# Moving group 4's attention output from TensorE to the crossbar, and groups 3 and 4 one unit earlier, in a fused window-attention and SwiGLU kernel

## The chip, the cores and the metric

The kernel runs on one core of one Trainium2 chip. The metric is the device time of one execution in microseconds (us), as the median of several runs. The kernel before takes 239.64 us (five runs, 239.41 to 241.12).

## The reference

Two layers are fused. The first is attention with a sliding window and attention sinks, for 4 batches, 8 heads, 768 tokens and a head width of 64. A query sees the first four keys of its sequence (the sinks) and the 128 most recent keys:

```python
keep = is_sink | in_window          # pos < 4, or 0 <= query - key < 128
a = softmax(where(keep, q @ k.T / 8, -1e9))
x = (a @ v) as [3072 tokens, 512]
```

The second is a SwiGLU block on these 3072 tokens, with a model width of 512 and an inner width of 1536:

```python
g = x @ w_gate
out = (g * sigmoid(g) * (x @ w_val)) @ w_out
```

## The kernel before

**Groups and blocks.** Attention runs over 12 groups of 256 tokens; group g is the third `g % 3` of batch `g // 3`. The SwiGLU block runs over eight token blocks of `SIZES` 256, 256, 256, 512, 512, 512, 512, 256 tokens. Block 3 holds groups 3 and 4, block 4 groups 5 and 6, block 5 groups 7 and 8, and so on. Blocks 0 and 1 share one 512-token buffer, under the name "01".

**The steps of a group g.**

- `load_nat(g)` (line 111) loads k and q in four DMAs from the POOL queue, `load_v(g)` (line 122) loads v in two. `NV(g)` is both. From group 4 on the loaded k and q lie in a buffer with a single copy (`natp`, one buffer), so that the load of the next group must wait until this group's k and q have been read.
- `xbar(g)` (line 259) reads them: four DMA transposes from the SP queue, through the crossbar, which write `kT` and `qT`. Groups 2 and 3 are transposed on TensorE instead (`TN`, line 245), groups 0 and 1 in other ways on TensorE.
- `Ss(g)` are two steps `step_S` (line 292): the scores of four heads each, 8 or 12 matmuls into four PSUM banks, four exponentials on ScalarE (line 299) and two masks on VectorE (line 304), which are put off until the next `flush`.
- `K(g)` is `step_K` (line 320): the scores against the sinks, for the groups that are not the first of their batch, and one exponential (line 324) that writes `es`.
- `PVs(g)` are four steps `step_PV` (line 355). The first one of a group that is not the first of its batch also issues the sinks' part for all four (line 335, `o<-vsb,es`), which reads `es`. VectorE then normalises (lines 363 and 369) into `xn`.
- `Xs(g)` are two steps `step_X`: 128 tokens of `xn` are transposed into `xT`, the input of the SwiGLU block. For groups in `PEX` TensorE does it in four matmuls (line 396, tile `px`) and VectorE or ScalarE copies the result; for the others it is one DMA transpose from the SP queue (line 391).

**Units.** The SwiGLU work is cut into units. A `gate` unit of a 512-token block is one slice f of 128 inner columns: four matmuls with the gate weights, a tanh on ScalarE, four matmuls with the value weights (all line 417), and two products on VectorE (lines 445 and 451). For a 256-token block a unit holds two slices, in matmuls of 256 columns. A `down` unit is 12 matmuls for 128 tokens (line 492), an eviction on ScalarE (line 497) and a store from the SP queue (line 500). In a gate unit the attention steps that are assigned to it come between the gate and the value matmuls; in a down unit they are spread over the 12 matmuls.

**The order is written by hand.** `weave` walks through a list of units and looks up each unit's attention steps in `slots`; a slot number is the index of the unit. Every engine works through its own instructions in this order, and so do the DMA queues of SP and POOL. The first weave holds the blocks 0, 1 and 2: slots 0 to 11 are the gates of blocks 0 and 1, 12 to 17 the gates of block 2, 18 and 19 the downs of block 0, 20 and 21 those of block 1, 22 and 23 those of block 2. The second weave holds block 3 (slots 0 to 11 gates, 12 to 15 downs), the third block 4, and so on. `pair(ga, gb)` places two groups in one weave.

Of the kernel before, what the change touches and what calls it, by code (L numbers as in the profile page):

```python
# [14 lines left out]
def kernel(  # L15
# [12 lines left out]
    nc = tc.nc  # L28
# [9 lines left out]
    DFC = DF // P  # L38
# [3 lines left out]
    SIZES = [256, 256, 256, 512, 512, 512, 512, 256]  # L42
    assert sum(SIZES) == NTOK and NG == 12
    OFF = [sum(SIZES[:i]) for i in range(len(SIZES))]
    PEX = (0, 1, 2, 4)

    VS = 72
    FCH = [2] * 6
# [108 lines left out]
    warmed = const.tile([P, 1], FP32)  # L157
# [49 lines left out]
    kTs, qTs, es_t, e_t, xns, xTs = {}, {}, {}, {}, {}, {}  # L207
# [171 lines left out]
    def step_X(g, j, evict="v"):  # L379
# [6 lines left out]
        elif tb > 1 and off == 0:  # L386
            xTs[tb] = dense(xtp.tile([P, DMC * 512], BF16, tag="xT", name="xT"),
                            DMC, SIZES[tb])
        if g not in PEX:
            def sp():  # L390
                nc.sync.dma_start_transpose(xTs[tb][:, :, off:off + P], xns[g, j])
# [110 lines left out]
    def gates(tb):  # L502
        return [(gate, tb, f) for f in range(0, DFC, 512 // SIZES[tb])]

    def downs(tb):
        return [(down, tb, t) for t in range(SIZES[tb] // P)]

    def A(fn, *a):
        return lambda: fn(*a)

    def TN(g, evict="av"):
        return [A(step_TN, g, i, j, evict) for j in range(2) for i in range(2)]

    def Ss(g):
        return [A(step_S, g, p2) for p2 in range(2)]

    def PVs(g):
        return [A(step_PV, g, j, hh) for hh in range(2) for j in range(2)]

    def Xs(g):  # L520
        return [A(step_X, g, j) for j in range(2)]

    def K(g):
        return A(step_K, g)

    def weave(us, slots):
        assert all(i < len(us) for i in slots)
        for i, (fn, tb, x) in enumerate(us):
            fn(tb, x, slots.get(i, []))

    def slots(*pairs):
        sl = {}
        for at, steps in pairs:
            for i, step in zip(at if isinstance(at, tuple) else (at,) * len(steps),
                               steps):
                sl.setdefault(i, []).append(step)
        return sl
# [81 lines left out]
    for i in range(4):  # L619
# [26 lines left out]
    flush()  # L646

    g0, g1, g2 = gates(0), gates(1), gates(2)
    us = [(gate_held, *g0[0][1:]), (gate_first, *g0[1][1:]), g1[0], g1[1], g0[2], g1[2],
          *((gate, "01", f) for f in range(6, DFC)),  # L650
          *g2, *downs(0), *downs(1), *downs(2)]

    def L(*fs):
        def f():
            for x in fs:
                x()
        return f

    def NV(g):
        return L(A(load_nat, g), A(load_v, g))  # L660

    weave(us, slots(
        (4, TN(2)[::2]), (5, TN(2)[1::2]), ((6, 7), Ss(2)), (6, [K(2)]),
        ((8, 8), PVs(2)[:2]), (9, [A(step_PV, 2, 0, 1, "a"), A(step_PV, 2, 1, 1, "a")]),
        ((10, 11), [A(step_X, 2, 0, "a"), A(step_X, 2, 1, "a")]),
        (11, [NV(4), lambda: nc.gpsimd.tensor_copy(out=vcl[64:128], in_=vcl[0:64])]),
        ((14, 14, 15, 15), TN(3, "aa")),
        (15, [A(xbar, 4)]), (15, [NV(5)]), (19, [A(xbar, 5)]), (19, [NV(6)]),
        (23, [A(xbar, 6)]), (23, [NV(7)]),
        ((17, 18), Ss(3)), (18, [A(step_ks, 1)]), (18, [A(step_vsb, 1)]),  # L670
        ((19, 19, 19, 20), PVs(3)), (20, Xs(3)),
        ((19, 20), Ss(4)), (19, [K(4)]),
        ((21, 21, 22, 22), PVs(4)), (22, Xs(4))))

    def pair(ga, gb, sh=0):
        s = sh
        return [((s, s + 2), Ss(ga)), (s, [K(ga)]),
                ((s + 4, s + 5, s + 6, s + 7), PVs(ga)),
                ((s + 6, s + 8), Ss(gb)), ((s + 8, s + 9), Xs(ga)), (s + 6, [K(gb)]),
                ((12, 12, 13, 13) if s else (10, 10, 11, 12), PVs(gb)),  # L680
                ((14, 14) if s else (12, 13), Xs(gb))]

    weave(gates(3) + downs(3), slots(
        (2, [A(xbar, 7)]), (2, [NV(8)]),
        (15, [A(step_ks, 2), A(step_vsb, 2)]), *pair(5, 6),
        (15, [A(xbar, 8)]), (15, [NV(9)])))
    weave(gates(4) + downs(4), slots(
        *pair(7, 8), (3, [A(xbar, 9)]), (15, [A(step_ks, 3), A(step_vsb, 3)]),
        (3, [NV(10)]), (15, [A(xbar, 10)]), (15, [NV(11)])))
    weave(gates(5) + downs(5), slots(*pair(9, 10), (6, [A(xbar, 11)])))  # L690
    us = gates(6) + gates(7) + downs(6) + downs(7)
    us[-1] = (lambda tb, t, a: down(tb, t, a, True), *us[-1][1:])
# [37 lines left out]
```

## Time and profile before

| | |
|---|---|
| median of 5 runs | 239.64 us |
| the profiled execution | 239.41 us |
| its span in the profile | 237.6 us (1.8 us lie around it) |
| mean TensorE clock granted | 0.998 of full speed |
| TensorE matmuls (PE) | 229.1 us busy, 96% of the span |
| VectorE (DVE) | 158.3 us, 67% |
| ScalarE (ACT) | 113.5 us, 48% |
| GpSimd (POOL), which issues the loads | 74.5 us, 31% |

Busy times are those of one profiled execution. Matmuls are pipelined and their ends are modelled, so the share of PE is an upper bound on its use. In the chain of waits each piece is either work or what released it; a DMA piece that runs beside busy TensorE costs only what is left when TensorE has run out of work. "Idle before" in the timeline is the time that an engine stood before an instruction, and the arrow names what ended it.

### The profile page before, as it was taken

How to read it: one execution, taken by the hardware profiler on the slowest of the kernel's cores; microseconds unless marked ns; L12 is line 12 of the kernel's file. 1: busy time of each engine (PE TensorE's matmuls, PEld its weight loads, DVE VectorE, ACT ScalarE, POOL GpSimd, SP SyncE). 2: the span in 40 equal slices, each digit the busy share in tenths (PEclk: the TensorE clock that was granted, in tenths of full speed). 3: DMA queues.
4: the chain of work that ended last, by engine and by line, in shares of the span. 5: the costliest groups of instructions: out<-in, count | busy, mean ns of one | idle time of the engine just before them, and what ended most of it. 6: DMA issues, size and time to landing. Idle time of an engine off the chain costs nothing.

```text
span 237.6 us, 4880 instructions
## 1 busy us (share of the span) xinstructions
PE 229.1 (96%) x1874; PEld 127.9 (54%) x1901; DVE 158.3 (67%) x336; ACT 113.5 (48%) x233; POOL 74.5 (31%) x98
## 2 busy tenths in 40 slices
PE   8899999999999999999999999999999999999994
PEld 5567845795555444543444454444444445488443
DVE  5887888768652888950798980588970598877000
ACT  4884485467443836412745622655622663333221
POOL 8996865720807117080352600080000000000000
PEclk9999999999999999999999999999999999999999
DMA  8999999996999999999498964599204100200132
GB/s 142 155 181 177 181 200 205 157 144 70 132 137 199 169 119 112 132 122 237 111 137 93 133 58 139 137 94 145 44 17 136 70 3 0 44 3 0 50 131 88
DMA packets 107655, 27.36 MB, mean 115 GB/s; under 512 B 94704, under 2 KB 104688, under 8 KB 107632
## 3 DMA queue, kind: packets, MB, share of 16 engines
q0 software_dynamic: 76640, 13.90, 76.9%
q1 hardware_dynamic: 30448, 12.89, 27.5%
q8 instruction: 15, 0.25, 0.4%
q10 hardware_dynamic: 544, 0.26, 0.4%
q14 instruction: 8, 0.07, 0.1%
HBM read 28.34 MB, written 6.29 MB: 146 GB/s over the span
## 4 chain that ended last, share of the span: by engine, by line
PE 84%; DMA 5%; ACT 3%; DVE 2%; POOL 2%; issue 2%; SPq 0%; POOLq 0%; DVEq 0%; ACTq 0%
PE pv L417 26%; PE pg L417 25%; PE pd L492 22%; PE o L355 4%; PE s L292 4%; DMA xT<-xn 3%; DMA va<-in_v_dram 2%; ACT e L299 2%; POOL rows L100 1%; DVE xn L369 1%; PE pn L245 1%; POOL x L188 1%; PE o L335 1%; PE pk L320 1%; ACT th L437 1%
## 5 line engine op out<-in xcount | busy, mean ns | idle before, releaser
L445 DVE SCALAR_TENSOR_TENSOR u<-th,pg 128x512 bf16<-128x512 f32 x72 | 49.1, 682 | 38.7 <-ACT th L437 38.7
L417 PE MATMUL pg<-xT,wg 128*128 128x512 bf16 (+1 forms) x351 | 73.1, 335 | 1.1 <-DMA xT<-xn 0.5
L437 ACT ACTIVATE th<-pg 128x512 f32<-128x512 f32 x72 | 43.5, 604 | 63.3 <-PE pg L417 59.6
L417 PE MATMUL pv<-xT,wv 128*128 128x512 bf16 (+1 forms) x351 | 73.1, 336 | 0.5 <-ACT e L299 0.2
L492 PE MATMUL pd<-wo,ht 128*128 128x512 bf16 (+2 forms) x291 | 64.8, 370 | 0.4
L451 DVE TENSOR_TENSOR ht<-u,pv 128x512 bf16<-128x512 bf16 x66 | 45.4, 687 | 9.8 <-PE pv L417 2.9
L417 PEld LDWEIGHTS <-wg 128*128 128x128 bf16 x360 | 35.1, 98 | 28.4 <-issue 1.3
L299 ACT ACTIVATE e<-s 128x512 bf16<-128x512 f32 (+1 forms) x88 | 42.9, 581 | 4.0 <-PE s L292 4.0
L492 PEld LDWEIGHTS <-ht 128*128 128x128 bf16 x300 | 27.9, 98 | 29.9 <-issue 0.5
L417 PEld LDWEIGHTS <-wv 128*128 128x128 bf16 x360 | 32.2, 98 | 20.5 <-issue 1.7
L111 POOL DMA_DIRECT2D nat<-in_k_dram x20 | 17.7, 888 | 76.1 <-DMA qT<-nat 73.7
L497 ACT ACTIVATE ot<-pd 128x512 f32<-128x512 f32 (+1 forms) x24 | 14.3, 596 | 47.4 <-PE pd L492 43.4
L304 DVE TENSOR_TENSOR e<-e,mask 128x1024 bf16<-128x1024 bf16 (+1 forms) x44 | 27.1, 649 | 4.0 <-ACT e L299 3.9
L122 POOL DMA_DIRECT2D va<-in_v_dram x24 | 21.5, 921 | 5.2 <-DMA wo<-in_moe_w_out_dram 2.5
L369 DVE TENSOR_TENSOR xn<-o,rcp 128x256 bf16<-128x256 f32 x45 | 19.1, 424 | 1.5
L355 PEld LDWEIGHTS <-e 128*128 128x128 bf16 x352 | 15.1, 98 | 8.0 <-DVE e L304 0.3
L111 POOL DMA_DIRECT2D nat<-in_q_dram x20 | 17.7, 898 | 1.0 <-DMA wv<-in_moe_w_val_dram 0.5
L355 PE MATMUL o<-va,e 128*128 128x65 bf16 x352 | 17.2, 194 | 0.4 <-DVE e L304 0.2
L292 PE MATMUL s<-qT,kT 64*128 64x128 bf16 (+1 forms) x240 | 12.9, 237 | 0.0
L292 PEld LDWEIGHTS <-kT 64*128 64x128 bf16 x240 | 7.7, 94 | 7.6 <-issue 6.6
L499 DVE TENSOR_SCALAR ot<-pd 128x128 f32<-128x128 f32 x1 | 0.3, 292 | 14.3 <-PE pd L492 14.3
L363 DVE RECIPROCAL rcp<-o 128x4 f32<-128x4 f32 x48 | 8.2, 174 | 1.7 <-PE o L355 1.7
(73 smaller groups left out, 91.6 us busy)
## 6 DMA issues: line engine op xcount, KB each, us to landing
out_dram<-ot SPq DMA_DIRECT2D x23, 256.0 KB
va<-in_v_dram POOLq DMA_DIRECT2D x24, 128.0 KB, 5.9
nat<-in_k_dram POOLq DMA_DIRECT2D x20, 128.0 KB, 4.7
nat<-in_q_dram POOLq DMA_DIRECT2D x20, 128.0 KB, 5.7
wg<-in_moe_w_gate_dram POOLq DMA_DIRECT2D x6, 256.0 KB, 8.0
wv<-in_moe_w_val_dram POOLq DMA_DIRECT2D x6, 256.0 KB, 8.3
wo<-in_moe_w_out_dram POOLq DMA_DIRECT2D x4, 384.0 KB, 11.1
st<-in_q_dram ACTq DMA_DIRECT2D x2, 128.0 KB
```

The costliest lines, as they stand in the source:

```text
L111: nc.gpsimd.dma_start(x[:, i, j].rearrange("p (h d) -> p h d", d=D), src[b, :, t0:t0 + P].rearrange("h p d -> p h d"))
L122: nc.gpsimd.dma_start(va[:, j, :, 0:D], v[b, :, t0:t0 + P].rearrange("h p d -> p h d"))
L292: nc.tensor.matmul(pss[2 * pp + h][:, col:col + n], kTs[b][r, p, kk:kk + P], qTs[b][r, p, qq:qq + n], start=True, stop=True)
L299: nc.scalar.activation(e_t[g][:, h0 + h, lo:512], pss[2 * pp + h][:, lo:512], AF.Exp, scale=scale)
L304: nc.vector.tensor_tensor(e, e, m[:, :, lo:512].broadcast_to([P, 2, 512 - lo]), op=ALU.mult)
L355: nc.tensor.matmul(o, l, r, start=(c == 0 and i == 0), stop=(i == len(mms) - 1), skip_group_check=True)
L369: nc.vector.tensor_tensor(xn, po[:, :, 0:D], rcp.broadcast_to([P, 4, D]), op=ALU.mult)
L417: nc.tensor.matmul(ps[:, i * n:(i + 1) * n], ws[fi][:, c, fo * P:(fo + 1) * P], xTs[tb][:, c], start=(c == 0), stop=(c == DMC - 1))
L437: nc.scalar.activation(th, pg, AF.Tanh, scale=0.5)
L445: nc.vector.scalar_tensor_tensor(u, th, 1.0, pg, op0=ALU.add, op1=ALU.mult)
L451: nc.vector.tensor_tensor(hts[tb][:, f:f + 512 // SIZES[tb]].rearrange("p a n -> p (a n)"), u, pv, op=ALU.mult)
L492: nc.tensor.matmul(po, hts[tb][:, f, ts * P:(ts + 1) * P], wos[f // n][:, f % n, lo:hi], start=(f == 0), stop=(f == DFC - 1))
```

## The change

- `PEX` loses group 4: its two output transposes become DMA transposes from the SP queue.
- In the first weave the units of slices 4 and 5 of blocks 0 and 1, each of two slices for one block of 256 tokens, become two joined units of one slice for 512 tokens.
- The steps of group 3 move up by one slot, those of group 4 by about one as well. The sink scores `K(4)` come directly after the second half of the scores of group 4, no longer after the first.
- `xbar(5)` with `NV(6)` moves from slot 19 to slot 22, so it comes after group 4's output. `xbar(6)` with `NV(7)` moves from slot 23 into slot 1 of the second weave, `xbar(7)` from slot 2 to slot 8 there.
- In the second weave the steps of group 5 and the scores of group 6 come one slot later. The value steps of group 6 go from slots 10, 10, 11, 12 to 10, 11, 11, 12, and its output stays in slots 12 and 13.
- `NV(8)` moves from slot 2 to slot 13. Ahead of it a new instruction on POOL reads one row of the last token of block 4's `xT`, so that POOL waits there for the transposed output of group 6.

```diff
-    PEX = (0, 1, 2, 4)
+    PEX = (0, 1, 2)
...
+    def behind(tb):
+
+        nc.gpsimd.tensor_copy(out=warmed[0:1], in_=xTs[tb][0:1, 0, 511:512])
...
-    us = [(gate_held, *g0[0][1:]), (gate_first, *g0[1][1:]), g1[0], g1[1], g0[2], g1[2],
-          *((gate, "01", f) for f in range(6, DFC)),
+    us = [(gate_held, *g0[0][1:]), (gate_first, *g0[1][1:]), g1[0], g1[1],
+          *((gate, "01", f) for f in range(4, DFC)),
           *g2, *downs(0), *downs(1), *downs(2)]
...
-        (15, [A(xbar, 4)]), (15, [NV(5)]), (19, [A(xbar, 5)]), (19, [NV(6)]),
-        (23, [A(xbar, 6)]), (23, [NV(7)]),
-        ((17, 18), Ss(3)), (18, [A(step_ks, 1)]), (18, [A(step_vsb, 1)]),
-        ((19, 19, 19, 20), PVs(3)), (20, Xs(3)),
-        ((19, 20), Ss(4)), (19, [K(4)]),
-        ((21, 21, 22, 22), PVs(4)), (22, Xs(4))))
+        (15, [A(xbar, 4), NV(5)]),
+        ((16, 17), Ss(3)), (18, [A(step_ks, 1), A(step_vsb, 1)]),
+        ((18, 18, 18, 19), PVs(3)), (19, Xs(3)),
+        (18, Ss(4)[:1]), (19, [L(Ss(4)[1], K(4))]),
+        ((20, 20, 21, 21), PVs(4)), (21, Xs(4)), (22, [A(xbar, 5), NV(6)])))
...
-                ((12, 12, 13, 13) if s else (10, 10, 11, 12), PVs(gb)),
-                ((14, 14) if s else (12, 13), Xs(gb))]
+                ((10, 11, 11, 12) if s else (10, 10, 11, 12), PVs(gb)),
+                ((12, 13), Xs(gb))]
...
-        (2, [A(xbar, 7)]), (2, [NV(8)]),
-        (15, [A(step_ks, 2), A(step_vsb, 2)]), *pair(5, 6),
-        (15, [A(xbar, 8)]), (15, [NV(9)])))
+        (1, [A(xbar, 6), NV(7)]), (8, [A(xbar, 7)]), *pair(5, 6, 1),
+        (13, [flush, A(behind, 4), NV(8)]),
+        (15, [A(step_ks, 2), A(step_vsb, 2), A(xbar, 8), NV(9)])))
```

## The prediction

> **What bounds the kernel now.** I read the page's busy times first, then the chain of waits, then the timelines of SP, POOL, PE and ACT around the moved steps.
>
> ```profile
> PE 229.1 (96%) x1874; PEld 127.9 (54%) x1901; DVE 158.3 (67%) x336; ACT 113.5 (48%) x233; POOL 74.5 (31%) x98
> PE 84%; DMA 5%; ACT 3%; DVE 2%; POOL 2%; issue 2%; SPq 0%; POOLq 0%; DVEq 0%; ACTq 0%
> ```
>
> TensorE is the bound. The span less PE's busy time is 8.5 us, but most of it is start and tail: the table of stages gives 0.23 us idle from 20 to 30 us, 0.25 from 58.5 to 62.9, 0.21 from 85 to 95, 0.52 from 101 to 112, 0.39 from 112 to 138, and about 2.6 us in all from 20 to 219 us. So a change that only hides waits can win some 2.6 us at most, and any new wait of PE is paid in full, because nothing later has slack to absorb it.
>
> The chain shows one large DMA piece, `105.21 6.71 DMA xT<-xn`, the last output transpose of group 6. The PE timeline tells what it costs:
>
> ```profile
> 101.84 9.66 PE L492 MATMUL pd<-wo,ht 128*128 128x512 bf16 x43
> 111.96 1.02 PE L417 MATMUL pg<-xT,wg 128*128 128x512 bf16 x4 [0.46 <-DMA xT<-xn]
> ```
>
> Four down units run under those 6.7 us; 0.46 us is left over. That wait is what holding back NV(8) can win.
>
> The change lives on two in-order DMA queues, so I took from them how long a crossbar step needs to land. First SP, then POOL, whose next load waits for the last of four transposes:
>
> ```profile
> 54.80 1.22 SPq L259 DMA_TRANSPOSE qT<-nat  x1
> 62.94 1.20 SPq L259 DMA_TRANSPOSE kT<-nat  x1
> 67.98 1.19 SPq L259 DMA_TRANSPOSE qT<-nat  x1
> 83.61 1.22 SPq L259 DMA_TRANSPOSE qT<-nat  x1
> 113.95 1.22 SPq L259 DMA_TRANSPOSE qT<-nat  x1
> ```
>
> ```profile
> 59.49 1.75 POOL L111 DMA_DIRECT2D nat<-in_k_dram  x2 [10.12 <-DMA qT<-nat]
> 72.84 1.75 POOL L111 DMA_DIRECT2D nat<-in_k_dram  x2 [8.11 <-DMA qT<-nat]
> 88.22 1.76 POOL L111 DMA_DIRECT2D nat<-in_k_dram  x2 [10.13 <-DMA qT<-nat]
> 116.96 1.76 POOL L111 DMA_DIRECT2D nat<-in_k_dram  x2 [11.17 <-DMA qT<-nat]
> ```
>
> From the issue of the last transpose to the release: 4.7 us (group 4), 4.9 (5), 4.6 (6), 3.0 (8). Four transposes with nothing to wait for issue 1.31 us apart. From a group's first load to the issue of its last transpose: 8.5 us (59.49 to 67.98), 10.8 (72.84 to 83.61), where three stores ran among them.
>
> **What the Trainium skill says.** "DMA: Bandwidth & Descriptors", section Issuing engines are not separate DMA queues: DMAs of all issuing engines run on the same 16 engines and interleave. The trace agrees: group 6's last transpose took 6.7 us beside NV(8)'s loads, where the uncrowded one of group 8 took 3.0. The same page, section Anatomy of one DMA: a DMA's wait is made on the issuing sequencer, before dispatch. It agrees: on SP, line 391 sat behind line 259's waits for loads. "TensorE: Matmul & The Clock Gate", section Part 4: a PE transpose takes about 275 ns in a kernel's context. In this trace four cost 0.22 us in the chain, 55 ns each, and I use that. Same page, Back-to-back issue gap: 262 cycles for 256 columns against 518 for 512, so joining two halves saves almost nothing; the trace's 0.87 us for eight and 0.86 for four agree.
>
> **The change part by part.** Sums are against the profiled execution, 239.41 us (237.6 and 1.8 around it), which stands 0.23 below the median.
>
> *Transposes of group 4 off PE.* 2 x 0.22 us: **-0.44**. Also two 0.42 us copies leave VectorE, which ends no wait there: 0. SP gets two transposes of 1.2 us each.
>
> *Joined units.* Eight passes, each 0.873 to 0.863 us: **-0.04** at most -0.1. VectorE's and ScalarE's instructions keep count and size. 0 for those.
>
> *Group 3 a slot sooner.* The scores in slot 16 need the copies of `TN(3)`, which end at 51.63 us; PE gets there at about 52.2. The masks of the second half end at about 57.85, and PE reaches the third value step at 57.84: 0 to 0.1. Slot 18 then holds one down bank, three value banks and four score banks, all eight of PSUM, so the next down bank may wait for a release: 0 to 0.5, I take **+0.1**.
>
> *Scores of group 4 a slot sooner.* Slot 18 starts at about 55.75 (before, 55.4; the second scores of group 3 now lie ahead of it). Ten down matmuls (2.16 us) and the value steps (0.48) put the first scores of group 4 at 58.4. The crossbar released group 4 at 59.49 by the POOL row, or 57.9 with group 8's 3.0 us. Wait 0 to 1.1, taken **+0.3**.
>
> *K(4) behind the second scores.* On ACT the four exponentials of 2.06 us now stand ahead of `es`. Before:
>
> ```profile
> 61.31 2.06 ACT L299 ACTIVATE e<-s 128x512 bf16<-128x512 f32 x4 [2.16 <-PE s L292]
> 63.24 0.31 ACT L324 ACTIVATE es<-pk 128x128 bf16<-128x128 f32 x1
> 65.13 2.06 ACT L299 ACTIVATE e<-s 128x512 bf16<-128x512 f32 x4 [1.09 <-PE s L292]
> ```
>
> There `es` was ready 3.3 us ahead of line 335 (66.87). Now: the second scores start at t, exponentials begin at t + 0.43 (61.31 less 60.88) and end at t + 2.5, `es` at t + 2.8. PE does scores 0.57, K 0.30, three matmuls 0.65, then four 0.86, and stands at the sink matmuls at t + 2.4. Wait **+0.45** (0 to 1). The gap of 0.25 before K(4) at 61.5 may close: **-0.1** (0 to -0.25).
>
> *Group 4's output by DMA.* Its last value step ends 8 down matmuls (1.73 us) ahead of slot 22, VectorE takes 0.65, the first transpose's issue 1.25: the second is issued some 5.6 us ahead of the first gate of block 3. It needs 3.1 to 4.9, with no load in the queues. **0**, hidden by the two downs of block 2; 6.7, the crowded value, would cost 1.1.
>
> *xbar(5) behind it.* SP's order is output, store of slot 21, xbar(5). The store waits for the eviction, 0.7 us after the slot's end E, and takes 0.5: the transposes start at E + 1.4, the last issues at E + 5.4, lands at E + 8.4 (3.0) or E + 10.3 (4.9). The scores of group 5, in slot 1 of the next weave, are due after two downs (5.18) and three passes of 0.86: E + 7.85. Wait **+0.55**, 0.3 to 2.4. Before, they had 3.6 us to spare (72.84 to 76.4).
>
> *NV(6), xbar(6).* POOL's loads start with that landing, 78.4 instead of 72.84; last transpose 8.5 to 9 later, landing 3.0 later: 90.2. The scores of group 6, now slot 7, are due at 91.3 (before 89.34, plus a unit of 1.73 and the shifts). Wait 0 to 2.4 (10.8 and 4.6 as group 6 had them); taken **+0.2**.
>
> *xbar(7), NV(8) and the POOL wait.* xbar(7) ends on SP near 101 (before 98.4); the outputs of groups 5 and 6 queue behind it, but the last is not ready until 103.8 anyway. It issues at 105.2 as before and lands in 3.1 uncrowded, 108.3, well ahead of 111.5: **-0.5** (0 to -0.5). POOL's one-element copy is free on its own; NV(8), NV(9) and later loads stand behind it. NV(8) starts near 108.6 instead of 100.54, so group 8 lands near 120.6; its scores are due at 125. The loads after it catch up: 0, the cover being this 4.6 us.
>
> Sum: -0.44 - 0.04 + 0.1 + 0.3 + 0.45 - 0.1 + 0.55 + 0.2 - 0.5 = +0.5, so 239.9 in a profiled execution and **240.0** as a median (half of the 0.23 added).
>
> **Rivals.** A measurement of this kernel can tell about 0.5%, 1.2 us, from no change.
>
> *The single k and q buffer gives slower.* One mechanism: xbar(5) queues behind group 4's output, so its landing frees the buffer some 5.6 us later for NV(6), and both score steps wait. For it: landings of 4.6 to 4.9 us for groups 4 to 6, 10.8 us of load and issue for group 6. Against it: the three stores that stretched group 6 don't recur. With 4.9, group 5 waits 2.4; with 10.8 and 4.6 from a start at 78.4, group 6 waits 2.4. One of them gives 241.9 to 242.2, both nearly 244. It decides once the two waits together pass 2 us; I put 242.1.
>
> *All new waits are hidden.* `es`, crossbars and banks cost nothing, and the old wait goes: -0.44 - 0.04 - 0.2 - 0.5 = -1.2, 238.2 to 238.4. For it: every new wait but one has a lower bound of 0. Against it: `es` comes after four exponentials in order.
>
> *Group 4's output lands late.* At 6.7 us it costs 1.1 at the second weave's start: 241.1 with the rest. Against it: no loads run beside it.
>
> *The hold does nothing*, because the 3 us are the crossbar's own: 240.5, within the bound.
>
> **Numbers.** The ledger's case, with the last rival, 0.52, own range 238.9 to 241.1; buffer 0.30 and late output 0.06 mostly above 240.85; hidden 0.12. Faster 0.12, same 0.52, slower 0.36. The range 238.5 to 242.4 takes in the hidden case and one late landing, and leaves out both at once.
>
> **What would show it.** Right: line 396 falls by 8 matmuls; PE waits at line 335 for `es` in slot 20; at line 292 for `kT<-nat` once or twice near 78 and 91; no wait of `pg` for `xT` at the third weave's start. Wrong: `pg` waits for `xT` near 75; group 5's scores start with no idle; waits for PSUM releases over 1 us in slots 18 to 20; or a wait at group 8's scores.

## The result, and the profile after

The changed kernel takes 239.58 us (median of 43 runs) beside 239.03 us of the kernel before (80 runs): a ratio of 1.0022, 95% interval 1.0013 to 1.0030, so 0.5 us slower. The forecast was 240.0 us and "same within 0.5%" as the likeliest case. It started from the five runs at 239.64 us; over 80 runs the kernel before came out 0.6 us lower, so it is the forecast difference, +0.5 us, that compares with the measured one. The profiled span went from 237.6 to 238.0 us. Four of the 22 executions of experiment 6 took 242.2 to 242.6 us, in a slow state whose cause no trace here shows, and are left out of its ratio.

The page of the changed kernel, first the busy times, then the chain's shares by engine:

```profile
PE 229.1 (96%) x1850; PEld 125.9 (53%) x1877; DVE 157.1 (66%) x334; ACT 113.8 (48%) x233; POOL 74.7 (31%) x99
PE 83%; ACT 4%; DMA 3%; SPq 3%; POOL 2%; issue 2%; DVE 2%; POOLq 0%; DVEq 0%; ACTq 0%
```

PE is as full as before, but DMA lost two points of the chain and SP's queue, 0% before, now has 3%. PE's timeline shows where PE stood (the last bracket is the idle time before, and what ended it):

```profile
64.37 0.29 PE L335 MATMUL o<-vsb,es 32*128 32x260 bf16 x4 [0.26 <-ACT es L324]
...
75.08 1.03 PE L417 MATMUL pg<-xT,wg 128*128 128x512 bf16 x4
...
78.89 0.56 PE L292 MATMUL s<-qT,kT 64*128 64x256 bf16 x10 [0.90 <-DMA qT<-nat]
...
92.32 0.51 PE L292 MATMUL s<-qT,kT 64*128 64x256 bf16 x8 [0.46 <-DVE rcp L363]
...
112.42 1.03 PE L417 MATMUL pg<-xT,wg 128*128 128x512 bf16 x4
```

The wait of 0.46 for group 6's output before the third weave is gone (112.42 has no bracket). In its place there are three: sinks of group 4 (0.26), scores of group 5 (0.90), scores of group 6 (0.46). The second weave starts at 75.08 us, where it started at 75.43 before:

```profile
75.43 1.03 PE L417 MATMUL pg<-xT,wg 128*128 128x512 bf16 x4
```

The third starts at 112.42, where it started at 111.96. Of the 0.35 us gained up to the second weave, 0.29 were there already at the last TensorE transposes of group 3 (49.58, before 49.87), and experiments 4 and 6 show that they are not the change's. So in these two profiles the moved steps of groups 3 and 4 gain 0.06 us, and the second weave loses 0.81.

The 0.06 us can't be told from nothing: from those transposes to the second weave PE took 25.56 us before and 25.50 after, but 25.76 and 26.17 in experiments 4 and 6, which have the same order as before in this stretch. The second weave is clearer. It takes 35.90 or 35.91 us in all five traces in which PE shows no wait for a transfer in it or at its end: experiments 2, 5 and 8, which have the changed order there, and 4 and 6, which have the order before. The changed kernel's 37.34 us is 1.4 us more, and it has two of the waits in it; the 36.53 us of the profile before is 0.6 us more, with one. So the new order of the second weave costs nothing of itself; its waits do.

The chain of waits of the changed kernel, in order of time, names the whole path into the 0.90 (columns: start, length, what):

```profile
68.59 0.42 DVE xn L369
69.02 0.08 DVE va L119
69.10 0.52 SPq L391
69.62 0.05 issue
69.72 1.22 SPq L391
70.93 0.04 issue
71.03 1.29 SPq L500
72.32 0.05 issue
72.41 1.23 SPq L259
73.64 0.05 issue
73.73 1.22 SPq L259
75.04 1.22 SPq L259
76.25 0.05 issue
76.35 2.51 DMA qT<-nat
78.89 0.56 PE s L292 x10
```

Read it backwards: group 5's scores wait for the landing of the fourth crossbar transpose; the four went out one behind the other; the first stood behind the store of slot 21 (line 500), which stood behind group 4's output (line 391). The one transfer in it, 2.51 us, is not a slow one: the same transpose took 2.5 us in experiments 1, 3 and 7 as well. The delay is that of one queue served in order.

### The profile page after: what moved, and what is told of

The parts are those of the page before. It is cut to its first block, busy times and chain, and to the rows that moved or that the text cites. A ratio compares the mean times of both kernels' runs of the same rounds, so it can differ in the third digit from the quotient of the medians.

```text
span 238.0 us, 4843 instructions
## 1 busy us (share of the span) xinstructions
PE 229.1 (96%) x1850; PEld 125.9 (53%) x1877; DVE 157.1 (66%) x334; ACT 113.8 (48%) x233; POOL 74.7 (31%) x99
## 4 chain that ended last, share of the span: by engine, by line
PE 83%; ACT 4%; DMA 3%; SPq 3%; POOL 2%; issue 2%; DVE 2%; POOLq 0%; DVEq 0%; ACTq 0%
PE pv L417 26%; PE pg L417 24%; PE pd L492 23%; PE s L292 4%; PE o L355 4%; ACT e L299 3%; DMA va<-in_v_dram 2%; SPq L259 2%; DMA qT<-nat 1%; POOL rows L100 1%; PE pn L245 1%; SPq L391 1%; POOL x L188 1%; PE o L335 1%; ACT th L437 1%
## 5 line engine op out<-in xcount | busy, mean ns | idle before, releaser
L451 DVE TENSOR_TENSOR ht<-u,pv 128x512 bf16<-128x512 bf16 x64 | 44.0, 687 | 11.0 <-PE pv L417 5.3
L417 PEld LDWEIGHTS <-wg 128*128 128x128 bf16 x352 | 34.3, 98 | 28.5 <-issue 0.6
L417 PEld LDWEIGHTS <-wv 128*128 128x128 bf16 x352 | 31.3, 98 | 20.8 <-issue 2.0
```

The lines of the kernel that those rows point to most:

```text
L417: nc.tensor.matmul(ps[:, i * n:(i + 1) * n], ws[fi][:, c, fo * P:(fo + 1) * P], xTs[tb][:, c], start=(c == 0), stop=(c == DMC - 1))
L451: nc.vector.tensor_tensor(hts[tb][:, f:f + 512 // SIZES[tb]].rearrange("p a n -> p (a n)"), u, pv, op=ALU.mult)
```

## The experiments

**1. The sink scores first.** The changed kernel, one line:

```diff
-        (18, Ss(4)[:1]), (19, [L(Ss(4)[1], K(4))]),
+        (18, Ss(4)[:1]), (19, [L(K(4), Ss(4)[1])]),
```

> The changed kernel with one edit: in slot 19 the sink scores of group 4 come ahead of the second half of its scores, not behind it. If the 0.26 us that TensorE waits at the sink matmuls of slot 20 come from the four exponentials ahead of es on ScalarE, es is ready some 1.5 us sooner, that wait goes, and the time falls by 0.2 to 0.35 us (239.2 to 239.4 where the changed kernel has 239.58); the waits of groups 5 and 6 at line 292 stay at about 0.9 and 0.5. Rival, a PSUM bank or VectorE is what holds the sinks: the wait stays, and the time with it.

Measured: ratio to the kernel before 1.0015 (0.9994 to 1.0035), against 1.0022 of the changed kernel: the 0.2 to 0.35 us that were expected can't be told from no gain. The wait at line 335 did go, so its cause is shown: on ACT `es` now ends at 62.5, ahead of the four exponentials. In PE's timeline the next wait grew:

```profile
64.25 0.29 PE L335 MATMUL o<-vsb,es 32*128 32x260 bf16 x4
...
79.10 0.56 PE L292 MATMUL s<-qT,kT 64*128 64x256 bf16 x10 [1.22 <-DMA qT<-nat]
```

The crossbar transposes of group 5 left SP no sooner (72.61, against 72.41), and PE's wait for them is 0.32 us longer. Group 6's scores (92.00) have no bracket here: their landing came sooner in this execution, though the loads of group 6 began 0.2 us later (79.61, against 79.41). In all, PE takes 25.01 us from group 3's last TensorE transposes to the second weave, against 25.50, and 37.30 for the second weave, against 37.34. So this trace has the gain of 0.26 us, with 0.16 more at group 4's scores, and it doesn't show it taken back; the ratio is too coarse to confirm it. The expectation that the other waits stay was wrong: they depend on when PE comes, and on landings that vary from execution to execution.

**2. Group 5's crossbar ahead of the store.**

```diff
-        ((20, 20, 21, 21), PVs(4)), (21, Xs(4)), (22, [A(xbar, 5), NV(6)])))
+        ((20, 20, 21, 21), PVs(4)), (21, Xs(4)), (21, [A(xbar, 5), NV(6)])))
```

> The changed kernel with group 5's four crossbar transposes (and the loads of group 6 behind them) at the end of slot 21, ahead of that slot's store on SP, not in slot 22 behind it. Theory of the single buffer and the SP order: the transposes start 1.2 to 1.4 us sooner, the 0.90 us wait at group 5's scores goes, the loads of group 6 start at about 78.0 instead of 79.4, and the 0.46 us wait at group 6's scores goes too: 1.2 to 1.4 us faster than the changed kernel, about 238.3, and 0.8 under the kernel before. Rival 1, the wait at group 6's scores is VectorE's (the trace names a reciprocal): only 0.9 goes, 0.46 stays. Rival 2, the crossbar is slow of itself: landing moves less than 0.5 us, and both waits stay.

Measured: ratio 0.9984 (0.9957 to 1.0011). By the two ratios that is 0.9 us under the changed kernel (the two intervals leave 0.05 to 1.7), less than the 1.2 to 1.4 that were expected; from the kernel before it can't be told. In the trace the second weave takes 1.43 us less. SP's timeline, then POOL's:

```profile
67.94 2.91 SPq L391 DMA_TRANSPOSE xT<-xn  x2
70.94 1.22 SPq L259 DMA_TRANSPOSE kT<-nat  x1
72.25 1.22 SPq L259 DMA_TRANSPOSE qT<-nat  x1
73.56 1.22 SPq L259 DMA_TRANSPOSE kT<-nat  x1
74.87 1.22 SPq L259 DMA_TRANSPOSE qT<-nat  x1
76.19 1.50 SPq L500 DMA_DIRECT2D out_dram<-ot  x3
```

```profile
77.97 1.75 POOL L111 DMA_DIRECT2D nat<-in_k_dram  x2 [15.83 <-DMA qT<-nat]
```

The transposes start 1.5 us sooner (70.94, not 72.41), group 6's loads 1.4 us sooner (77.97, not 79.41), and PE waits at neither score step: 77.55 and 90.55 have no bracket. For group 5 that settles the cause: PE came to its scores only 0.21 us sooner (77.55, against 77.76).

For group 6 it settles less. PE came to these scores 1.3 us sooner, too, and the last transpose of group 6 left SP 1.25 us sooner (86.70, against 87.95). What opened the gap is that the release came quicker after it: POOL went on 4.5 us after that issue, not 5.0. Yet the reciprocal on VectorE, which the trace of the changed kernel names, is not what these scores wait for. In experiment 1 they start before it has ended (92.00, against 92.09):

```profile
91.91 0.18 DVE L363 RECIPROCAL rcp<-o 128x4 f32<-128x4 f32 x1
...
92.00 0.50 PE L292 MATMUL s<-qT,kT 64*128 64x256 bf16 x8
```

So it was the landing of group 6 that PE waited for, which comes by way of the single buffer, since POOL starts the loads of group 6 only when group 5's transposes release it. But whether the wait is there at all depends on a landing that varies by half a microsecond: it is one execution's 0.46.

**3. Without the hold.** The changed kernel, with group 8's loads right behind group 7's transposes:

```diff
-        (1, [A(xbar, 6), NV(7)]), (8, [A(xbar, 7)]), *pair(5, 6, 1),
-        (13, [flush, A(behind, 4), NV(8)]),
+        (1, [A(xbar, 6), NV(7)]), (8, [A(xbar, 7), NV(8)]), *pair(5, 6, 1),
```

> The changed kernel without the hold: no POOL instruction behind group 6's output, and the loads of group 8 right behind the transposes of group 7 (slot 8). If those loads slow group 6's last output transpose as in the kernel before, it lands 2 to 4 us later than the 110.8 us of the changed kernel, and TensorE, which needs it at 112.4, waits 0.4 to 2 us at the third weave's first gate: 0.4 to 2 us slower. Rival, the transpose is not slowed: no wait there, same time within 0.1.

Measured: ratio 1.0177 (1.0136 to 1.0217). The direction held, the size did not: PE waits 3.4 us (PE timeline).

```profile
115.99 1.04 PE L417 MATMUL pg<-xT,wg 128*128 128x512 bf16 x4 [3.40 <-DMA xT<-xn]
```

Group 6's last output transpose left SP at 108.61 and released PE at 115.99, 7.4 us later; the loads of group 8 were issued from 105.06 to 110.3. And there is an after-effect. The table by stage (columns: stretch, its length, busy time and count of PE, PEld, DVE, ACT and POOL, granted clock, DMA share, GB/s):

```profile
116.00:117.00 1.00, 1.00 (x6) 0.34 (x8) 0.00 (x0) 0.00 (x0) 0.00 (x0) 0.98 1.31 327
117.00:118.00 1.00, 1.00 (x17) 0.64 (x20) 0.31 (x1) 0.94 (x2) 0.00 (x0) 0.50 1.42 173
118.00:119.00 1.00, 1.00 (x10) 0.35 (x11) 0.38 (x1) 1.00 (x3) 0.00 (x0) 0.50 1.30 148
119.00:120.00 1.00, 1.00 (x4) 0.35 (x3) 0.00 (x0) 0.83 (x3) 0.00 (x0) 0.50 1.33 260
```

The clock granted is half for at least 3 us, which by estimate (half of 3 us) costs some 1.5 us more than the wait. It is not in every execution: four of the six have a mean clock of 0.991 to 0.993 and take 243.2 to 245.0 us, the other two a mean clock of 1.0 and 242.0 and 242.5 us.

**4. The hold alone**, on the kernel before (`behind` is added as in the change):

```diff
-        (2, [A(xbar, 7)]), (2, [NV(8)]),
+        (2, [A(xbar, 7)]),
...
+        (13, [flush, A(behind, 4), NV(8)]),
```

> The kernel before with the hold alone: the loads of group 8 move from slot 2 to slot 13 of the second weave, behind a POOL read of block 4's last token; nothing else. If the hold is what removed the 0.46 us wait of TensorE for group 6's output, this kernel is 0.4 to 0.5 us faster than before (about 238.6), with the loads of group 8 starting near 108.5 and group 8's scores not waiting. Rival, the later loads make group 8 late: a wait at its scores near 125 us takes the gain back, same or slower.

Measured: ratio 0.9981 (0.9966 to 0.9996), 0.45 us faster (0.1 to 0.8 by the interval), as expected. No wait is left at the third weave's first gate. Group 8's loads start at 108.60, after the POOL read at 107.57. So one part of the change, taken alone, is a gain. The same hold is worth 0.45 us in the order before and some 3.7 us in the changed order (1.0177 less 1.0022; the two intervals leave 2.5 to 4.9), since there group 7's transposes, and with them group 8's loads, come later, next to group 6's output.

**5. Group 4 back on TensorE**, the rest as changed:

```diff
-    PEX = (0, 1, 2)
+    PEX = (0, 1, 2, 4)
```

> The changed kernel with group 4's two output transposes back on TensorE. My ledger has the transposes as 0.44 us of gain and the SP queue behind them as the loss. If SP's order is the loss, the crossbar of group 5 starts 2 us or more sooner (near 70 instead of 72.4), the waits at the scores of groups 5 and 6 (0.90 and 0.46) go, 0.44 of transposes come back: 0.8 to 0.95 us faster than the changed kernel, about 238.7. Rival: the waits come from moving xbar(5) to slot 22, not from the two transposes ahead of it; then SP issues it at the same time, the waits stay, and the kernel is 0.4 slower than the changed one.

Measured: ratio 0.9989 (0.9971 to 1.0007), 0.8 us under the changed kernel by the two ratios (their intervals leave 0.1 to 1.4), as expected. The transposes of group 5 left SP at 71.57, only 0.84 us sooner and not the 2 us expected: the store of slot 21 waits for its eviction in any case. It was enough. No bracket is left at the scores of groups 5 and 6, in part because PE arrives later by the 0.44 of the transposes (78.18 at group 5's scores). Moving the transposes off TensorE, in this order of SP, bought 0.44 us and cost more. The 0.44 can be seen apart here: from group 3's last TensorE transposes to the second weave PE takes 25.78 us, against 25.34 in experiment 2, whose work for PE in this stretch differs by these eight matmuls alone.

**6. Joined units alone**, on the kernel before:

```diff
-    us = [(gate_held, *g0[0][1:]), (gate_first, *g0[1][1:]), g1[0], g1[1], g0[2], g1[2],
-          *((gate, "01", f) for f in range(6, DFC)),
+    us = [(gate_held, *g0[0][1:]), (gate_first, *g0[1][1:]), g1[0], g1[1],
+          *((gate, "01", f) for f in range(4, DFC)),
```

> The kernel before with the joined units of slices 4 and 5 alone. By the durations of the passes this is worth 0.04 us, at most 0.1: not to be told from the kernel before (ratio within 0.002 of 1). Rival: fewer, longer matmuls free the weight loads or the exponentials of the units around them, and 0.3 us or more are won.

Measured: ratio 1.0002 (0.9984 to 1.0020). Nothing to be told from the kernel before, as expected. The last TensorE transposes of group 3 start at 49.64 here, at 49.58 in the changed kernel, and at 49.53 in experiment 4, which has no joined units; the 0.3 us by which all three lie ahead of the profile before (49.87) is therefore not theirs.

This trace also shows that the wait for group 6's output comes and goes in the order before. There is none at the third weave's first gate here; there is one at the second weave's, for the output of group 3, whose transposes left SP from 68.47 us on, while the loads of group 6 were issued from 69.62:

```profile
75.81 1.02 PE L417 MATMUL pg<-xT,wg 128*128 128x512 bf16 x4 [0.45 <-DMA xT<-xn]
```

In the changed order the output of group 3 leaves SP from 61.86 us on, and the loads of group 6 begin at 79.41; no trace of that order has this wait. The forecast didn't count that gain.

**7. Two buffers for loaded k and q**, the rest as changed:

```diff
-    natp = pool("natp", 1)
+    natp = pool("natp", 2)
```

> The changed kernel with two buffers for loaded k and q, not one; order of everything as it is. The loads of group 6 then start in slot 22 near 71 us, not at 79.4. If the single buffer is why group 6 waits, the 0.46 us wait at its scores goes; group 5's wait (0.90), which comes from SP's order, stays, and grows by up to 2 us if the loads of group 6 now slow group 5's crossbar transposes. Sum: between 0.5 us faster and 1.5 us slower than the changed kernel. Rival, the wait of group 6 is VectorE's (the reciprocal that the trace names): it stays.

Measured: ratio 1.0318 (1.0288 to 1.0347), 7 us slower than the changed kernel and far outside what I expected. The wait of group 6 did go, but a new one opened where I had expected none, at group 4's scores (PE timeline, then POOL's):

```profile
63.67 0.93 PE L292 MATMUL s<-qT,kT 64*128 64x256 bf16 x10 [4.60 <-DMA qT<-nat]
...
85.75 0.56 PE L292 MATMUL s<-qT,kT 64*128 64x256 bf16 x10 [1.05 <-DMA qT<-nat]
```

```profile
49.43 1.75 POOL L111 DMA_DIRECT2D nat<-in_k_dram  x2
51.16 1.77 POOL L111 DMA_DIRECT2D nat<-in_q_dram  x2
52.89 1.79 POOL L122 DMA_DIRECT2D va<-in_v_dram  x2
```

With a second buffer nothing holds group 5's loads back. They run from 49.43 instead of 58.95, beside group 4's four transposes, whose last one leaves SP at 54.49 and releases PE at 63.67: 9.2 us; in the changed kernel that transpose left at 54.46 and POOL went on at 58.95, 4.5 us later. After the 4.6 us wait the table by stage has PE's clock at 0.57 from 63 to 66 us. The single buffer delays, and it is also a hold: it keeps the next group's loads off this group's transposes.

**8. Experiments 1 and 2 together**, on the changed kernel.

```diff
-        (18, Ss(4)[:1]), (19, [L(Ss(4)[1], K(4))]),
-        ((20, 20, 21, 21), PVs(4)), (21, Xs(4)), (22, [A(xbar, 5), NV(6)])))
+        (18, Ss(4)[:1]), (19, [L(K(4), Ss(4)[1])]),
+        ((20, 20, 21, 21), PVs(4)), (21, Xs(4)), (21, [A(xbar, 5), NV(6)])))
```

> Both edits on the changed kernel: the sink scores ahead of the second scores of group 4, and group 5's crossbar transposes in slot 21 ahead of the store. If the waits are independent the gains add: 0.26 and 1.36 of wait gone, some 1.3 to 1.6 us under the changed kernel, 238.0 where the kernel before has 239.3 on this chip (ratio 0.995 to 0.998). Rival, one eats the other: PE is only earlier at the same landing of a load or transpose, and the ratio is that of the second edit alone, 0.998.

Measured: 238.36 us beside 239.36 of the kernel before, ratio 0.9968 (0.9951 to 0.9985); span 236.0. It beats the changed kernel by 1.3 us (0.7 to 1.9 by the two intervals), as expected, and the kernel before by 0.8 us (0.4 to 1.2). PE's timeline has no bracket at the sinks nor at either score step:

```profile
63.85 0.29 PE L335 MATMUL o<-vsb,es 32*128 32x260 bf16 x4
...
77.24 0.62 PE L292 MATMUL s<-qT,kT 64*128 64x128 bf16 x12
...
90.22 0.51 PE L292 MATMUL s<-qT,kT 64*128 64x256 bf16 x8
```

The edit whose gain could not be told by itself (1) shows in the trace here: PE is 0.31 us ahead of experiment 2 at the sinks and still at group 5's scores (77.24 against 77.55). The two ratios differ by 0.16% and their intervals overlap, so the rival, that the second edit does it all, is not excluded by the times.

## Why the prediction was right

The forecast, "same", and its sum (+0.5 us, measured +0.5) held, and the mechanism of the ledger, new waits on an SP queue that is served in order against the transposes and the old wait that go, is the one that the chain shows. The size of the sum is in part luck. Term by term, the waits by one profile each:

| term | forecast, us | measured, us | shown by |
|---|---|---|---|
| output transposes off PE | -0.44 | -0.44; 8 matmuls fewer at line 396 (24, before 32) | experiments 2 and 5 |
| joined units | -0.04 | ratio 1.0002 alone | experiment 6 |
| PSUM release in slot 18 | +0.1 | no such wait in the trace | profile |
| group 4's scores at its crossbar | +0.3 | PE row 0.16 longer than its like (0.78, 0.62); not so in experiments 1, 2, 5 and 8, a wait of 0.66 in experiment 3 | profile |
| `es` behind the exponentials | +0.45 | +0.26 | experiment 1 |
| gap before K(4) | -0.1 | -0.25, no bracket at line 320 | profile |
| group 5's scores | +0.55 | +0.90 | experiment 2 |
| group 6's scores | +0.2 | +0.46; none in experiment 1 | profile |
| wait for group 6's output | -0.5 | -0.46 (0.45 alone, 0.1 to 0.8); no such wait in experiment 6 either | experiment 4 |

- *The place of each wait* was right: `es` at line 335 in slot 20, two waits at line 292, none before the third weave. The second weave was worked out to start 5.6 us after the second output transpose is issued, enough for it, and no wait of `pg` for `xT` is there.
- *Terms that were mis-sized.* Group 5's wait came out 0.35 too small. The store of slot 21 was priced at 0.5 us of SP and took 1.29, so the transposes left at 72.41; that was partly made up, since PE was released 2.5 us after the last issue and not 3.0. Group 6's wait grew from two sides: the loads began at 79.41 and not at 78.4, and the last transpose took 4.4 us to release PE and not 3.0, while PE was due at 91.86 and not at 91.3. The early terms erred the other way (PSUM 0.1, group 4's scores 0.14, `es` 0.19, the gap 0.15 too dear), so the errors nearly cancelled: the measured column adds up to +0.6, the ratio says 0.5 (0.3 to 0.7). By stage the same shows: the terms up to the second weave were to cost 0.27 us together, and the profiles show -0.06; those of the second weave were to cost 0.25, and the profiles show 0.81. A right sum is not nine right terms.
- *The cover of 4.6 us for group 8* was enough, but less was left of it. Group 6's last output transpose was to be issued at 105.2 us and left SP at 108.20, and the loads of group 8 were to start near 108.6 and started at 111.86 (SP's row, then POOL's):

```profile
108.20 1.23 SPq L391 DMA_TRANSPOSE xT<-xn  x1
110.82 0.18 POOL L525 CAST warmed<-xT 1x1 f32<-1x1 bf16 x1 [12.60 <-DMA xT<-xn]
111.86 1.76 POOL L111 DMA_DIRECT2D nat<-in_k_dram  x2 [0.86 <-DMA out_dram<-ot]
```

The transpose landed 1.6 us ahead of the third weave (112.42), where 3.2 had been worked out. Group 8's transposes let POOL go on at 123.78, 2.55 us ahead of its scores (126.33), and PE has no wait there.
- *A reading of the profile before*: not four down units run under the 6.7 us of group 6's transpose, since one takes 2.6 us, but about two and a half. The 0.46 us that was left over is read from the trace and stands. And two downs and three passes, 5.18 and 2.58 us, add up to 7.76, not 7.85; the slip is 0.09.
- *The single-buffer rival* had the mechanism right and the dose too high: the two waits together came to 1.36 us, under the 2 us from which it would have decided. What made it small was a landing near 2.5 us for group 5 and 4.4 for group 6.
- *The rival "the hold does nothing"* is refuted by experiments 3 and 4. The rival that hides all new waits is refuted by the three in the trace, and that of a late output of group 4 by the second weave's first gate, which has no wait at 75.08.
- *Not settled*: why the landing of the fourth transpose varies. Group 4's, with the same instructions ahead of it, let POOL go on at 58.95 in the changed kernel and at 56.89 in experiment 2, 4.5 and 3.0 us after its issue. In the changed kernel the DMA engines stand idle meanwhile (share 0.00 to 0.01 from 56.5 to 59 us), so the bytes seem to have been moved 2.4 us before the release; what it then waited for the traces don't show.

## What to carry to other kernels

When PE is the bound, a step that is moved off it is paid for on the queue that it moves to: ask what stands behind it there, and follow that to the next PE step that needs it. On an in-order DMA queue put the transfer that gates the next stage ahead of stores that nobody waits for; here one slot was worth 0.9 us by the ratios of experiment 2 and the changed kernel. Look for transfers that are kept apart by accident, by a single buffer for example, before adding buffers, and keep them apart on purpose where they meet: a hold of one POOL instruction took 0.45 us (0.1 to 0.8) off the kernel before. And where waits hang on landings that vary, one profile shows which waits are possible, and many runs show what they cost.

## What the runs showed of the hardware

- A wait of PE of 3.4 us (experiment 3) or 4.6 us (experiment 7) is followed by about 3 us at a granted clock near half in these two traces. The Trainium skill, "TensorE: Matmul & The Clock Gate", section Why this matters for your kernels, asks for no idle gaps over some 3 us. The traces agree as far as they go: a wait of 1.22 us (experiment 1) and one of 0.90 (the changed kernel) are followed by a clock of 1.00, and no trace here has a wait of PE between these and 3.4 us.
- Beside loads issued from POOL, a crossbar transpose needed 6.7 us (before), 7.4 (experiment 3) and 9.2 (experiment 7) from issue to release, against 2.5 for group 5 in the changed kernel, where no loads ran beside it. Group 6 took 4.4 there, with the last packets of its own loads still under way at its issue. That loads lengthen it is shown by experiments 3, 4 and 7; they need not be the only cause.
- On one landing PE goes on sooner than POOL: group 5's released PE at 78.89 and POOL's next load began at 79.41, and the distance is 0.5 us in experiments 1, 3 and 7, too. A landing that is read off POOL's timeline, as in the prediction, is about 0.5 us late for PE.
